# phi of q before the transpose instead of after it, w1 of the first expert by contraction chunks, and a new written-out order for the first stage of a linear-attention and mixture-of-experts kernel

## The chip, the cores and the metric

The kernel runs on one core of a Trainium2 chip. A core has five engines that run side by side and wait for each other by semaphores: TensorE (PE; matrix products, results in PSUM), VectorE (DVE), ScalarE (ACT), GpSimd (POOL) and SyncE (SP). Transfers between HBM and SBUF are issued by SP, ACT or POOL and carried by 16 DMA engines. The metric is the device time of one execution in microseconds (us); lower is better. Each engine has a list of instructions of its own in the program and works through it in order, so an instruction that waits holds up what stands behind it on its engine.

## The reference

The first half is a linear attention over q, k, v of 8 batches, 8 heads, 576 positions and 64 features; the second is a mixture of 8 experts over the 4608 rows that come out, in which every expert works on every row and a balanced routing matrix weighs them.

```python
def phi(x):
    return np.where(x > 0, x, np.exp(x) - 1.0) + 1.0
q_p, k_p = (phi(q), phi(k))
kv = np.einsum('bhsd,bhse->bhde', k_p, v)
z = np.sum(k_p, axis=2)
num = np.einsum('bhsd,bhde->bhse', q_p, kv)
den = np.einsum('bhsd,bhd->bhs', q_p, z)[..., None] + 1e-06
...
logits = x @ w_gate                       # x: (4608, 512), the attention's output
P = np.exp(logits - logits.max())
for _ in range(8):                        # rows, then columns
    P /= P.sum(1, keepdims=True) + 1e-09
    P /= P.sum(0, keepdims=True) + 1e-09
    P *= N / E
for e in range(8):
    h = np.maximum(x @ w1[e], 0.0)        # 512 -> 1024
    out += P[:, e:e + 1] * (h @ w2[e])    # 1024 -> 512
```

phi(x) is computed as min(exp(x), max(x + 1, 1)): one exp on ACT, one tensor_scalar (add, max) and one tensor_tensor (min) on DVE.

## The kernel before, in words

**Stages.** The attention is done in 16 units, one for each batch and group of four heads; unit n is `att(b, g)`, n = 2b + g. A unit loads its parts of k, q and v as tiles of 128 x 1152 elements (L350; k stays fp32, q and v are cast to fp16 by the transfer), makes phi of k (L360, L364, L368), multiplies it with v in 18 matmuls of a 64-row half of the array each (`kv_ps`, L384) and copies the result into the tile `kvz` (L310 on ACT, L312 on DVE). For q it first transposes: 18 matmuls against the identity (L411), each with 64 columns of weights and 128 moving columns, whose results fill 64 of the 128 partitions of the PSUM tile `att`, so that two of them make one 128 x 128 transpose. Then exp (L415, ACT, reading PSUM), max (L418, DVE, reading PSUM) and min (L421, DVE) make `qpT`, phi of q transposed. From qpT and kvz come the denominators (`att`, L434; ACT then takes Ln, L447, and Exp of the negative, L452) and the numerators (`num_ps`, L434), and their product (L462, DVE) is written to `xT`, the transposed x, in fp16.

The experts work on blocks g of 512 rows, nine of them. For expert 0 the blocks 0 to 4 are done plainly (`unit_plain`, `layer1`): 32 matmuls of 512 columns for x @ w1 (`hq`, L635), relu (L640, L642), 32 more for h @ w2 (`ye`, L863) and a copy of the result (L310, L312, L879, L881). Block 0 does its first four pieces of w1's columns in two halves of the contraction: `jobs` in `layer1` lists pieces 0 to 3 with the first two of four 128-row chunks, then the same pieces with the last two, then pieces 4 to 7 whole. Blocks 5 to 8 of expert 0 and all blocks of experts 1 to 7 but the last use a seven-product scheme (`block7`, `unit`), for which sums of blocks of xT are formed (`x_blocks`, L675 to L680) and stored, with xT itself, to a DRAM tile `xd` (L691, L661, L662), from which later experts read them (L708).

As soon as rows of xT are there, the plain blocks of expert 0 are the work with which PE fills the time that the attention leaves. After the last of the four groups of logits (L478) comes the routing: eight iterations on DVE with one small matmul each (L517), also beside expert 0. 46 matmuls of zeros (`yw`, L551) run at the very start; they compute nothing that is used.

**Order.** `_Plan` is a planner inside the kernel: every step is added with an engine, a cost, dependencies and the buffers that it takes, and the planner emits the instructions. For the first stage the planner does not choose: `_FRONT` is a list, written out by hand or by a search, of step numbers with a letter for the engine (p PE, a ACT, d DVE, g POOL, s SP, m a transfer, n nothing), and the steps are emitted in that order. After the list's end it picks by earliest start and priority. Dependencies that the planner knows order the emission only; what an instruction waits for on the chip follows from the tiles that it reads and writes.

**Buffers and queues.** k, q and v have three buffers each (`NK`, `NQ`, `NV`), so a load of unit n waits until the readers of the buffer's previous content are done: for q those are the transposes (PE), for v the 18 kv matmuls (PE), for k the exp and max (ACT and DVE). All loads but the first k go through POOL's queue, in order, with at most eight under way (`p_sw`): the ninth waits for the landing of the first. `att` has two PSUM banks, shared by transposes, denominators, logits and the small routing matmuls; `kv_ps` and `num_ps` share one buffer. The weights of expert 0 are loaded in two parts each (L287): w1 by halves of its 1024 columns, each half in two transfers of 64 partitions, w2 by halves of its contraction. The stores of block sums of the first five blocks (L691) leave from two halves of the tile `acc6` (`p_xse`).

Of the kernel before, what the change touches and what calls it, by code (L numbers as in the profile page):

```python
# [11 lines left out]
FP16 = mybir.dt.float16  # L12
AF = mybir.ActivationFunctionType
ALU = mybir.AluOpType
# [3 lines left out]
class _Plan:  # L18
# [121 lines left out]
    1n 102g 103m 117n 106n 583n 48s 49m 2p 3p 50g 51m 4p 52g 53m 5p 6p 75g 76m 7p 8p 79g 80m 9p 10p 77g 78m 55d 54a  # L140
    11p 12p 124g 125m 13p 14p 15p 0g 16p 56d 17p 18p 126g 127m 19p 20p 21p 61n 107g 108m 62p 109g 110m 22p 63a 23p
    24p 57n 151g 152m 58p 64d 65d 25p 59a 26p 81a 27p 153g 154m 60d 82d 66p 28p 29p 67a 83d 30p 128g 129m 31p 32p 68p
    84n 85p 69a 88n 112g 113m 89p 86d 87a 90a 71p 131d 155g 156m 33p 34p 35p 70a 36p 91d 37p 38p 114g 115m 39p 40p
    92d 130a 41p 42p 43p 72d 93p 178g 179m 44p 94a 45p 73p 46p 74d 137n 95p 111n 180g 181m 96a 132d 100p 47p 97a 138p
    182g 183m 158d 584p 139a 101d 585p 586p 118g 119m 157a 587p 140d 98p 99d 164n 165p 133n 121g 122m 159d 134p 166a
    141d 205g 206m 588p 135a 167d 590p 136a 592p 589d 160n 207g 208m 142p 591d 161p 143a 168d 116n 209g 210m 144p
    162d 594p 145a 163d 596p 234g 235m 185d 146a 169p 597d 147p 598p 170a 148d 236g 237m 600p 184a 599d 595d 171p
    238g 239m 149p 172a 602p 186d 191n 593a 150d 187n 192p 620n 603d 188p 193a 120n 104g 105m 606p 189d 173a 194d
    604p 195d 190a 601a 176p 123n 261g 262m 196p 177d 605p 197a 607p 612d 211a 263g 264m 212d 198p 174p 199a 608p
    213d 218n 290g 291m 200a 175d 219p 265g 266m 214n 215p 220a 621p 216a 221d 292g 293m 217a 240a 623p 222d 622d  # L150
    201p 614a 223p 609p 202d 224a 241d 624a 203p 225p 247n 625p 204d 317g 318m 226a 242d 228p 227a 232p 243n 627p
    626a 229d 233a 267a 268d 248p 230p 249a 319g 320m 629p 231d 274n 344g 345m 296a 610p 250d 321g 322m 251d 244p
    628a 616a 630d 275p 297d 611p 276a 346g 347m 269d 348g 349m 631p 270n 245a 277d 371g 372m 246a 633p 323a 278d
    252p 632d 271p 253a 634a 254p 272d 294g 295m 635p 255a 273d 324d 641p 256a 653n 325d 279p 257p 280a 654p 258d
    636a 281p 618d 259p 282a 656p 655d 303n 326n 283a 260d 304p 657d 284p 305a 402g 403m 298d 642p 400g 401m 285d
    639p 649a 306d 286p 330n 287d 299n 331p 307d 300p 332a 373g 374m 658p 301d 377a 302d 660p 333d 350a 351d 308p
    327p 661d 309a 334d 659a 310p 431g 432m 640p 328d 311a 378d 427g 428m 662p 312a 329d 481g 482m 352d 315p 335p
    664p 316d 336a 647a 313p 337p 314d 357n 637p 338a 569d 638p 339a 663d 340p 358p 341d 665d 643p 359a 342p 666p
    360d 384n 353n 343d 385p 361d 354p 386a 668p 404g 405m 355a 387d 645a 456g 457m 644p 356a 667d 669a 375g 376m
    570d 362p 379d 686n 687p 363a 571d 651a 670p 388d 572s 573m 688a 367p 364p 689p 365a 672p 366a 691p 406a 368d  # L160
    673p 548d 692a 380n 369p 680a 288p 370d 413n 407d 381p 289a 433a 408d 454g 455m 414p 382d 409n 549d 676p 415a
    429g 430m 383d 434d 483g 484m 671p 487a 416d 677p 417d 690a 389p 555d 410p 390a 435d 391p 411d 693p 392a 412d
    678d 396p 393a 418p 550d 695p 419a 397d 674p 556d 420p 557d 394p 421a 675p 558s 559m 395d 440n 436n 551s 552m
    422a 461d 441p 560s 561m 694d 437p 442a 696d 574s 575m 697p 438d 458g 459m 439d 485g 486m 699p 443d 698a 425p
    700a 398p 426d 444d 701p 399a 684a 682a 445p 719n 423p 446a 720p 424d 467n 460a 447p 488d 452p 703p 490g 489d
    448a 538n 544n 539g 540m 705p 462d 449a 541g 542m 702d 463n 468p 545g 546m 453d 706p 469a 450p 721a 722p 470d
    495n 491n 451d 724p 471d 496p 464p 497a 704p 723a 498d 465a 726p 725d 466a 713d 472p 492p 499d 473a 727d 474p
    493a 728p 562d 475a 494a 563d 709p 476a 711d 500p 576d 477p 501a 710p 478d 502p 729d 479p 503a 707p 480d 504a
    708p 505p 715a 730p 506d 732p 717d 577d 507p 731d 733a 742p 508d 734p 536n 756d 509p 763n 578d 757d 736p 735d
    510a 752d 737p 758d 753d 759s 760m 537p 744a 553s 554m 764p 754d 740p 765a 755d 778p 511d 768p 743p 769a 770p  # L170
# [21 lines left out]
    749d 1156a 1163p 1136d 1165p 1135d 1164a 1161p 1132d 1126a 1167p 1166d 1162a 1127g 1200p 1168d 1202p 1201a 1125g  # L192
    1137p 1203a 1169p 1139d 1199n 1206p 1138d 1170a 1254s 1255m 1208p 1207a 1171d 1204p 1175p 1172d 1177p 1173d 1176a
    1205a 1174d 1180p 1178d 1179d 1210p 1181a 1185p 1211d 1188p 1187d 1186d 1212p 1209d 1214p 1213a 1216p 1215a 1191p
    1217a
"""


# [914 lines left out]
```

## Time and profile before

| | us |
|---|---|
| median of the timed runs (three: 972.72, 970.70, 972.14) | 972.14 |
| the profiled execution | 972.0 |
| its span, first to last instruction | 970.2 |
| PE busy in the span | 957.8 (99%) |
| DVE, ACT, POOL busy | 774.8, 566.0, 145.6 |
| PE idle in the first 200 us | 6.6 |
| last load of q, k or v landed at | 113.8 |
| first matmul of expert 1 | 198.2 |

The span and what lies around it make the profiled execution's time; a sum that is made against the profile therefore starts from 972.0. Busy PE is not PE at its peak: a matmul is counted from its start to its modelled end and overlaps the next. How long a group really holds PE is read from the start of its first matmul to the start of the next group's first.

### The profile page before, as it was taken

The numbers are of one execution on the slowest core, as the hardware profiler recorded it, in microseconds if no ns is written. First come the engines' busy times: TensorE is split into PE (matmuls) and PEld (weight loads), VectorE is DVE, ScalarE is ACT, GpSimd is POOL, SyncE is SP. The second block draws the span as 40 slices with busy tenths as digits, with TensorE's granted clock in tenths as the row PEclk, the third lists the DMA queues.
The fourth block names the chain that finished last, engine by engine and source line by source line (L and its number), as shares of the span: only waits on it lengthen the run. The fifth ranks groups of instructions, "written<-read, shape, count | busy, mean of one in ns | idle before, by whom it ended". The sixth has DMA issues, their size and how long they took to land.

```text
span 970.2 us, 21138 instructions
## 1 busy us (share of the span) xinstructions
PE 957.8 (99%) x8624; PEld 796.5 (82%) x8624; DVE 774.8 (80%) x1481; ACT 566.0 (58%) x1004; POOL 145.6 (15%) x209
## 2 busy tenths in 40 slices
PE   8999999999999999999999999999999999999998
PEld 4555566688888888888888888888888888888886
DVE  5897888887887888878887888878887888877775
ACT  6896745555655555555555555555555555555553
POOL 6432100002112111111112111111112111111110
PEclk9999999999999999999999999999999999999999
DMA  9997665023526322272226322272225322236554
GB/s 215 257 227 164 150 179 185 1 77 95 146 77 130 106 74 73 74 160 74 74 76 141 95 74 77 76 161 77 77 77 134 106 78 76 77 99 164 163 164 109
DMA packets 46193, 112.52 MB, mean 116 GB/s; under 512 B 4368, under 2 KB 26640, under 8 KB 46096
## 3 DMA queue, kind: packets, MB, share of 16 engines
q1 hardware_dynamic: 21056, 75.57, 24.0%
q0 software_dynamic: 24640, 35.07, 19.2%
q8 instruction: 67, 1.10, 0.5%
q10 hardware_dynamic: 400, 0.52, 0.2%
q14 instruction: 30, 0.25, 0.1%
HBM read 119.69 MB, written 17.69 MB: 142 GB/s over the span
## 4 chain that ended last, share of the span: by engine, by line
PE 90%; DMA 4%; DVE 3%; ACT 1%; issue 1%; POOL 1%; DVEq 0%; ACTq 0%; POOLq 0%
PE ye L981 33%; PE hq L757 23%; PE att L757 12%; PE Zye L757 6%; PE ye L863 6%; PE Zye L981 5%; DMA vv<-in_v_dram 4%; PE hq L635 2%; PE kv_ps L384 1%; DMA kin<-in_k_dram 1%; DVE h L792 1%; PE att L411 1%; DVE acc L995 1%; PE att L434 1%; PE num_ps L434 1%
## 5 line engine op out<-in xcount | busy, mean ns | idle before, releaser
L995 DVE SCALAR_TENSOR_TENSOR acc<-ye,P_sb,acc 128x256 f32<-128x256 f32 x620 | 267.4, 479 | 125.5 <-PE ye L981 124.9
L757 PEld LDWEIGHTS <-W 128*128 128x128 f16 x2144 | 209.7, 98 | 29.1 <-issue 2.2
L981 PEld LDWEIGHTS <-S 128*128 128x128 f16 x1984 | 193.9, 98 | 23.9 <-DVE S L954 1.4
L1005 POOL TENSOR_TENSOR acc<-acc,st 128x256 f32<-128x256 f32 x124 | 88.1, 730 | 701.1 <-ACT st L1002 583.3
L981 PE MATMUL ye<-T,S 128*128 128x256 f16 x1488 | 192.8, 273 | 0.2 <-DVE S L954 0.2
L757 PEld LDWEIGHTS <-w 128*128 128x128 f16 x1608 | 157.3, 98 | 21.1 <-issue 0.8
L789 ACT ACTIVATE h<-hq 128x512 f16<-128x512 f32 x134 | 80.1, 598 | 149.3 <-PE hq L757 146.0
L981 PEld LDWEIGHTS <-h 128*128 128x128 f16 x1488 | 145.6, 98 | 17.4 <-issue 0.5
L757 PE MATMUL att<-xs,W 128*128 128x256 f16 x1008 | 151.2, 273 | 0.4 <-DVE h L792 0.2
L757 PE MATMUL hq<-xs,W 128*128 128x256 f16 x1008 | 151.2, 273 | 0.0
L757 PE MATMUL hq<-xs,w 128*128 128x256 f16 x1008 | 140.9, 273 | 0.3 <-DVE h L792 0.3
L786 ACT ACTIVATE h<-Zye 128x512 f16<-128x512 f32 x134 | 80.1, 598 | 39.8 <-PE Zye L757 39.8
L792 DVE CUSTOM_DVE_ANT_0 h<-att,s 128x512 f16<-128x512 f32 x126 | 86.6, 687 | 13.1 <-ACT s L776 12.1
L1002 ACT ACTIVATE st<-Zye,P_sb 128x256 f32<-128x256 f32 x124 | 52.3, 470 | 76.2 <-PE Zye L981 76.1
L776 ACT COPY s<-hq 128x512 f32<-128x512 f32 x126 | 73.5, 583 | 35.3 <-PE hq L757 35.2
L954 DVE TENSOR_TENSOR S<-h 128x1024 f16<-128x1024 f16 x124 | 85.2, 687 | 10.9 <-ACT h L789 10.9
L769 ACT COPY Zye<-hq 128x512 f32<-128x512 f32 x134 | 77.8, 581 | 23.3 <-PE hq L757 23.2
L792 DVE CUSTOM_DVE_ANT_0 h<-hq,s 128x512 f16<-128x512 f32 x126 | 86.6, 687 | 3.5 <-PE hq L757 3.3
L863 PE MATMUL ye<-w,h 128*128 128x512 f16 x312 | 76.7, 382 | 0.3 <-DMA w<-in_moe_w_dram 0.2
L783 ACT COPY s<-att 128x512 f32<-128x512 f32 x126 | 74.5, 591 | 2.3 <-PE att L757 1.5
L757 PE MATMUL Zye<-xs,w 128*128 128x256 f16 x504 | 75.6, 273 | 0.0
L981 PE MATMUL ye<-w,S 128*128 128x256 f16 x496 | 64.3, 273 | 0.7 <-DVE S L954 0.7
(102 smaller groups left out, 947.9 us busy)
## 6 DMA issues: line engine op xcount, KB each, us to landing
xs<-xd SPq DMA_DIRECT2D x63, 896.0 KB, 4.6
kin<-in_k_dram POOLq DMA_DIRECT2D x15, 576.0 KB, 8.3
out_dram<-acc SPq DMA_DIRECT2D x67, 128.0 KB, 2.4
w<-in_moe_w_dram POOLq DMA_DIRECT2D x16, 512.0 KB, 8.7
w<-in_moe_w_dram POOLq DMA_DIRECT2D x7, 1024.0 KB, 13.3
qin<-in_q_dram POOLq DMA_DIRECT2D x16, 288.0 KB, 7.4
vv<-in_v_dram POOLq DMA_DIRECT2D x16, 288.0 KB, 8.1
xd<-acc SPq DMA_DIRECT2D x5, 512.0 KB, 3.7
```

The source lines that it names most:

```text
L757: nc.tensor.matmul(dst[:, p, :], lhsT=lhs(p, c), rhs=rhs(c), start=(first and p == 0 and c == 0), stop=(c == 1), skip_group_check=True)
L769: nc.scalar.copy(out=Zt[1], in_=gX["tile"])
L776: nc.scalar.copy(out=gs2["tile"], in_=gX["tile"])
L783: nc.scalar.copy(out=gs5["tile"], in_=gR["tile"])
L786: nc.scalar.activation(out=hd(0, 0), in_=Zt[1], func=AF.Relu)
L789: nc.scalar.activation(out=hd(1, 0), in_=gX["tile"], func=AF.Relu)
L792: nc.vector._custom_dve(TENSOR_ADD_SAT, out=dst, in0=ps, in1=sb, s0=3.0e38, s1=0.0)
L863: nc.tensor.matmul(gy[tt]["tile"], lhsT=gh["tile"][:, f, ds(P * tt, P)], rhs=gw2["tile"][:, f, :], start=(f == 0), stop=(f == NFT - 1))
L954: nc.vector.tensor_tensor(out=Sx[:, i], in0=a0, in1=a1, op=op)
L981: nc.tensor.matmul(bank(g_)[:, s, :], lhsT=lhs(s, kk), rhs=rhs(kk), start=(new and s == 0 and kk == 0), stop=(kk == 3), skip_group_check=True)
L995: nc.vector.scalar_tensor_tensor(out=dst(), in0=bank(g_)[:, s, :], scalar=P_sb[:, gg, e:e + 1], in1=dst(), op0=ALU.mult, op1=ALU.add)
L1005: nc.gpsimd.tensor_tensor(out=dst(), in0=dst(), in1=gst["tile"], op=ALU.add)
```

## The change

Four things change.

1. **phi of q.** exp, max and min are now done on q as it was loaded, [128 x 2 x 9 x 64] in SBUF; the result `tq` holds the two heads of a pair side by side, so that one transpose takes a full 128 x 128 block: nine matmuls for each unit instead of 18. The transposed result is copied from PSUM to `qpT` by ACT or DVE. k's and q's exp share one tile of three buffers.
2. **First w1.** The first expert's w1 is loaded by the four 128-row chunks of the contraction, one transfer of 128 partitions each, in place of the halves of its columns. Block 0's first four half-contraction pieces depend on the first two chunks, all other pieces on all four.
3. **Block sum stores.** In the planner, the store of a block's sums depends on the landing of all loads of q, k and v.
4. **A new `_FRONT`.** The list is replaced as a whole. In the program that comes out, PE does 31 of the 46 zero matmuls before its first other work (before: 20), and POOL issues two more v and q loads ahead of the first w1 transfer, and 14 of the 16 copies to `qpT` are DVE's, two ACT's. From the first blocks of expert 1 on, PE's order is the same in both kernels (13961 of its rows, weight loads counted).

The core of the diff; the planner's cost entries that change with it and the list itself are cut.

```diff
-    1n 102g 103m 117n 106n 583n 48s 49m 2p 3p 50g 51m 4p 52g 53m 5p 6p 75g 76m 7p 8p 79g 80m 9p 10p 77g 78m 55d 54a
+    1n 106g 107m 108n 119n 599n 48s 49m 2p 3p 50g 51m 4p 0g 5p 6p 52g 53m 7p 8p 76g 77m 9p 78g 79m 10p 11p 54a 55d
...
-    p_ek, p_eq, p_t, p_kvz, p_qpT, p_rden = (S_.pool(2) for _ in range(6))
+    p_t, p_tq, p_kvz, p_qpT, p_rden = (S_.pool(2) for _ in range(5))
+    p_ek = p_eq = S_.pool(3)
...
     def load_w1(e, parts=1, **kw):
-        n = F // parts
-        return load_w(moe_w1, "w1", p_w1, [[((slice(64 * r, 64 * r + 64), slice(None), slice(n * i, n * i + n)),
-                                             256 * F * r + n * i, [[F, PW], [PW * F, NDT], [1, n]]) for r in range(2)]
-                                           for i in range(parts)], e, shape=[P, NDT, F], **kw)
+        if parts > 1:
+            return load_w(moe_w1, "w1", p_w1, [[((slice(None), c), PW * F * c, [[256 * F, 2], [F, PW], [1, F]])
+                                                for c in (2 * i, 2 * i + 1)] for i in range(2)], e, shape=[P, NDT, F], **kw)
+        return load_w(moe_w1, "w1", p_w1, [[((slice(64 * r, 64 * r + 64),), 256 * F * r, [[F, PW], [PW * F, NDT], [1, F]])
+                                            for r in range(2)]], e, shape=[P, NDT, F], **kw)
...
+        all_land.extend(tin.values())
...
         def f_qt(_):
             for j in range(NJ):
-                for r in range(2):
-                    nc.tensor.transpose(at2.rearrange("p a b -> p (a b)").bitcast(FP16)[64 * r:64 * r + 64, P * j:P * j + P],
-                                        gin["q"]["tile"][:, r, j, :], ident)
+                nc.tensor.transpose(at2.rearrange("p a b -> p (a b)").bitcast(FP16)[:, P * j:P * j + P],
+                                    gtq["tile"][:, j].rearrange("p r d -> p (r d)"), ident)
...
         def f_qe(_):
-            nc.scalar.activation(out=geq["tile"], in_=qps(), func=AF.Exp)
+            nc.scalar.activation(out=geq["tile"], in_=gin["q"]["tile"], func=AF.Exp)
 
         def f_qm(_):
-            nc.vector.tensor_scalar(out=gq["tile"], in0=qps(), scalar1=1.0, scalar2=1.0, op0=ALU.add, op1=ALU.max)
+            nc.vector.tensor_scalar(out=gtq["tile"].rearrange("p j r d -> p r j d"), in0=gin["q"]["tile"], scalar1=1.0, scalar2=1.0, op0=ALU.add, op1=ALU.max)
 
         def f_qp(_):
-            nc.vector.tensor_tensor(out=gq["tile"], in0=gq["tile"], in1=geq["tile"], op=ALU.min)
...
+            tv = gtq["tile"].rearrange("p j r d -> p r j d")
+            nc.vector.tensor_tensor(out=tv, in0=tv, in1=geq["tile"], op=ALU.min)
+
+        def f_qc(e):
             gq["tile"] = fp.tile([P, 2, NJ, PW], FP16, tag="qpT", name="qpT")
-        t0 = fadd(("none", 0.0), f_qa, deps=[tin["q"], t_id[0]], acq=[gq, geq], prio=pr)
-        t1 = fadd(("pe", 0.626), f_qt, deps=[tin["q"], t0], acq=ga, use=[gin["q"]], prio=pr, cfg=2)
-        t2 = fadd(("act", 1.14), f_qe, deps=[t1], use=[*ga, geq], prio=pr)
-        t3 = fadd(("dve", 0.76), f_qm, deps=[t1, t2], use=[*ga, gq], prio=pr)
-        tq = fadd(("dve", 0.76), f_qp, deps=[t2, t3], use=[geq, gq], prio=pr)
+            copy(e, gq["tile"], qps())
+        gtq = S_.grp(p_tq)
+        t0 = fadd(("none", 0.0), f_qa, deps=[tin["q"]], acq=[gtq, geq], prio=pr)
+        t2 = fadd(("act", 1.16), f_qe, deps=[t0], use=[gin["q"], geq], prio=pr)
+        t3 = fadd(("dve", 0.5), f_qm, deps=[t0], use=[gin["q"], gtq], prio=pr)
+        tm = fadd(("dve", 0.76), f_qp, deps=[t2, t3], use=[geq, gtq], prio=pr)
+        t1 = fadd(("pe", 0.52), f_qt, deps=[tm, t_id[0]], acq=ga, use=[gtq], prio=pr)
+        tq = fadd({"act": 1.13, "dve": 0.76}, f_qc, deps=[t1], acq=[gq], use=[*ga, gq], prio=pr)
...
-            t1 = add(("pe", 0.2175 * (c1 - c0)), f_hq, deps=[tw1[f // 4], prev_hq[0]] + xd_[0:c1 if g == 0 else None],
+            t1 = add(("pe", 0.2175 * (c1 - c0)), f_hq, deps=[tw1[0 if c1 == 2 else 1], prev_hq[0]] + xd_[0:c1 if g == 0 else None],
...
-        ti = add(("sp", 0.45), f_st, deps=[last], use=[gt_], prio=0.0)
+        ti = add(("sp", 0.45), f_st, deps=[last] + all_land, use=[gt_], prio=0.0)
```

## The prediction

> **What bounds the kernel now.** I read the page's first two parts, then the busy time by stretches of the first stage, then the timelines of PE, POOL and SP there, and last the groups of the operations that change. The page first: PE's row, its clock, and DMA.
>
> ```profile
> PE 957.8 (99%) x8624; PEld 796.5 (82%) x8624; DVE 774.8 (80%) x1481; ACT 566.0 (58%) x1004; POOL 145.6 (15%) x209
> ...
> PEclk9999999999999999999999999999999999999999
> DMA  9997665023526322272226322272225322236554
> ```
>
> PE is the bound throughout; from the first blocks of expert 1 (198.2 us) its order is the same in both kernels. So the question is how much earlier or later PE gets there. The stretches of the first 200 us (columns: busy us of PE, PEld, DVE, ACT, POOL, then PE's granted clock, DMA share, GB/s):
>
> ```profile
> 0.00:40.00 40.00, 36.09 (x309) 19.03 (x310) 28.10 (x46) 26.51 (x32) 22.64 (x38) 1.00 1.09 225
> 40.00:70.00 30.00, 29.35 (x320) 17.10 (x319) 25.75 (x40) 27.71 (x37) 10.76 (x15) 1.00 1.10 262
> 70.00:130.00 60.00, 58.60 (x555) 32.75 (x550) 47.83 (x84) 42.75 (x59) 11.02 (x15) 0.97 0.70 146
> 130.00:200.00 70.00, 69.35 (x493) 46.56 (x490) 59.51 (x135) 36.11 (x66) 0.00 (x0) 1.00 0.35 113
> ```
>
> PE is idle for 3.9, 0.65, 1.4 and 0.65 us, 6.6 in all; up to 40 us the DMA engines are full. DVE and ACT have least room at 40 to 70 us, 53.5 of 60. One undisturbed transpose block on PE, and PE's longest wait after the start:
>
> ```profile
> 101.73 1.03 PE L863 MATMUL ye<-w,h 128*128 128x512 f16 x4
> 102.69 0.69 PE L411 MATMUL att<-ident,qin 128*64 128x128 f16 x18
> 103.31 0.92 PE L384 MATMUL kv_ps<-vv,t 64*128 64x192 f16 x18
> ```
>
> ```profile
> 88.81 1.04 PE L478 MATMUL att<-wg_sb,xT 128*128 128x8 f16 x36
> 91.04 1.22 PE L384 MATMUL kv_ps<-vv,t 64*128 64x192 f16 x18 [1.18 <-DMA vv<-in_v_dram]
> 92.18 1.17 PE L411 MATMUL att<-ident,qin 128*64 128x128 f16 x18
> 93.29 3.56 PE L863 MATMUL ye<-w,h 128*128 128x512 f16 x12
> ```
>
> What made that v late (POOL's and SP's queues):
>
> ```profile
> 81.28 0.72 POOL L350 DMA_DIRECT2D vv<-in_v_dram  x1 [7.62 <-PE kv_ps L384]
> 82.00 0.74 POOL L350 DMA_DIRECT2D qin<-in_q_dram  x1
> 82.72 0.74 POOL L350 DMA_DIRECT2D vv<-in_v_dram  x1
> ...
> 84.01 18.69 SPq L691 DMA_DIRECT2D xd<-acc  x3
> ```
>
> POOL stood 7.6 us for a v buffer, then issued three loads at once; a 512 KB block-sum store joined at 84.01. The three landed at 85.62, 88.83 and 90.99, 3.2 and 2.2 us apart, where full queues land one each 1.4 us earlier on. The groups that change, over the first 200 us:
>
> ```profile
> L418 DVE TENSOR_SCALAR qpT<-att 128x1152 f16<-128x1152 f16 x16 | 12.1, 755 | 9.5 <-ACT eq L415 9.3
> L421 DVE TENSOR_TENSOR qpT<-qpT,eq 128x1152 f16<-128x1152 f16 x16 | 12.0, 752 | 0.2
> L364 DVE TENSOR_SCALAR t<-kin 128x1152 f16<-128x1152 f32 x16 | 12.0, 752 | 2.5 <-DMA kin<-in_k_dram 2.4
> L415 ACT ACTIVATE eq<-att 128x1152 f16<-128x1152 f16 x16 | 18.0, 1126 | 12.6 <-PE att L411 12.6
> L551 PE MATMUL yw<-warm 128*128 128x512 f16 x46 | 13.6, 442 | 1.3 <-DVE warm L540 1.3
> L411 PE MATMUL att<-ident,qin 128*64 128x128 f16 x288 | 11.6, 227 | 0.5 <-DVE qpT L418 0.4
> ```
>
> **The change part by part.** *Transposes.* The block starts at 102.69 and the next group at 103.31: 0.62 us for 18. The four 512-column matmuls before it began at 101.73 and hold PE 0.86 (86.84 to 87.70 for such four), up to 102.59: another 0.10 lost on entry. A unit so pays 0.72. Now nine matmuls with 128 moving columns and full weights: at 0.215 for 512 columns, 0.054 each, 0.48 a block. Loading full weights allows more: the logits' 36 matmuls with full weights take 0.88 us, 0.024 each. Lower end: each full one takes as long as the pair it replaces (0.069), 0.62, and the entry stays: no gain. Upper end: 0.48, no entry, 0.24. I take 0.50 without entry, since full-array groups follow each other without such a gap in the rows: 0.22 x 16 = 3.5 us less (0 to 3.8). All of it is PE work, hence on the path.
>
> A rule speaks against this. The Trainium skill ("TensorE: Matmul & The Clock Gate", Part 4) gives about 275 ns for a full 128x128 bf16 transpose in a kernel's context. By that figure as a spacing the nine would take an estimated 2.5 us and the sum would be some 28 us worse; the trace has 227 ns as one transpose's duration too, but starts them 34 ns apart.
>
> *phi of q.* exp stays on ACT (1.126 from PSUM; L360 reads SBUF in 1.157: +0.03). Max reads SBUF in place of PSUM: L364, same form with fp32 input, 0.752, so 0 saved, half of it (0.38) at best. Min is 0.752 as before. The copy is new: on DVE at most the 0.755 that L418 takes for the same PSUM source, on ACT 1.13. So DVE gains 14 x 0.755 = 10.6 us of work less 0 to 6, ACT 2.3; four relu and two copies move from DVE to ACT in the new list (-4.1, +3.5). On PE's path this costs nothing while other PE work stands between a transpose and its denominator: at least an hq block and a num (1.1 us) in the new order, mostly 2 to 4 us, against 0.1 + 0.755. Without that cover each unit shows up to 0.76. What leaves the path: between transpose and denominator lay 1.126 + 0.755 + 0.752; the two att banks come free earlier, and a q buffer waits no more for PE (POOL's 11.5 us of waits for att go).
>
> *Start.* Issue for issue: 31 zero matmuls end at 10.4 (20 ended at 8.0, a later one takes 0.216), so the first kv starts at 10.5 instead of 9.51 and the first denominator, after the copy, at about 13.2 instead of 12.09. POOL makes the identity ahead of its second load (0.55 later) and puts v2 and q3 before w1 (0.7 of POOL each); behind w1, k of unit 3 lands at 25.9 instead of 21.45 and its kv comes at 28.4 instead of 27.68. With 1.4 us a load, w1's first two chunks (512 KB each, priced 1.4) land at 20.3 and 21.7, all four at 24.5; before, the first half landed at 20.17, all at 28.42. PE comes to its first hq at 22.1 instead of 21.51, but with unit 2's kv done (0.9 us, before at 24.54). w2's halves land at 34.3 and 37.0 (before 35.40 and 37.95, and PE waited 0.18 there). At the kv of unit 5, PE is 1.4 us further on, of which the transposes are 1.0: 0.4 gained. Between -1 and +1.5: the chunks could land as slowly as the 2.04 and 2.09 apart of the old ones.
>
> *Store behind the last load.* This holds in the planner alone. On the chip SP waits for DVE's sums and nothing else, so the first store leaves when DVE has made them, still beside the last v loads; what is stored is first read for expert 1, whose work starts at 198 us. I cost it at nothing; a collision costs the load behind it up to 2.6 us (3.2 + 2.2 - 2 x 1.4). DVE's fourth and fifth early sums wait for a store's landing (3.7 us), with over ten DVE instructions between.
>
> *Stalls.* The wait before 91.04 cost 1.3 us. Behind it the clock was halved for 3.4 us (the profile's 0.97): kv 1.14 to the next start instead of 0.86, the block 1.11 instead of 0.62 and 0.2 of gaps, twelve ye 3.39 instead of 2.58: 1.8. The new order has its own such place: units 9 and 10 use the same v buffer one after the other. Between their kv groups PE has 5.9 us; a load takes 4.2 to 4.9 when POOL's queue is quiet (63.63 to 67.85, 70.74 to 75.63), and up to two loads at 1.4 go ahead: 4.9 to 7.7, so a wait of 0 to 1.9, and with a halved clock 1.8 more. I take 0.9 for the wait and 1.8 for the clock, net 0.4 gained; the ends are 3.1 gained and 1.5 lost.
>
> The Trainium skill (same page, Part 1) says that an idle stretch of about 3.4 us halves the clock. By that a wait of 1.2 us would cost itself alone, and this term would be 2.2 gained. Here 0.9 us of 8-column matmuls and 1.2 idle were enough, so the row decides.
>
> *Sum.* 3.5 + 0.4 + 0.4 = 4.3. The profiled execution's 972.0 becomes 967.7; the median is 0.14 above it: **967.8**.
>
> **The rivals.** *No long wait at all* (every v early): 972.1 - 3.5 - 0.4 - 3.1 + 0.5 for small ones = 965.6. For it: q loads are freed from PE, so POOL's queue moves earlier. Against: the shared v buffer.
>
> *Eaten by the new order:* the wait at units 9 and 10 in full (1.9 + 1.8 against the old 3.1) and as much as 3.5 us of PE waits for tq, which now has to be ready before the transpose instead of after it: 972. For it: an in-order PE has one more DVE result to wait for in each unit. Against: q lands well ahead once its buffer goes free early.
>
> *Slower, DVE and ACT become the bound of the attention.* They are 89% busy at 40 to 70 us; some 4.3 units fall there, and a copy of 0.755 each makes 56.7 of 60. In two in-order engines at 94% each late item waits for PE and PE for it. The 16 copies are 12.9 us; if two thirds come out as PE idle, +8.6 - 3.9 = 976.8, if all, 981. It decides from a third on (4.3 us). Against: over 70 to 130 us the two have 29 us free, the new order moves work to ACT, and DVE's 9.3 us of waits for exp and ACT's 12.6 for the transposes are gone.
>
> *The transposes do not run side by side with their own latency:* nine at 227 ns, 2.04 instead of 0.72, x16: 993. Against: the 34 ns of today. The Trainium skill's 275 ns, named above, is the rule behind it.
>
> That the store change does nothing on the chip is in the sum already.
>
> **How the numbers follow.** A measurement of this kernel can tell about 0.2% (1.9 us) from no change. The forecast (965.9 to 970) has 0.48, no long wait 0.20, eaten 0.13, slower 0.17, slow transposes 0.02. Faster 0.68, same 0.13, slower 0.19. The range reaches from the best ends (3.8 + 1.5 + 3.1 = 8.4 less, 963.7) to 975.5, inside the slower case, leaving out its upper half and the last one; within it, the forecast's own is 965.9 to 970.
>
> **What would show it.** Right: transposes at nine in about 0.50 us with no gap ahead; DVE's waits for exp fall; first hq near 22; expert 1's first matmul near 194; few PE waits over 0.5 us after 40 us. Wrong: PE waiting for DVE's tq or qpT in most units (slower case); a wait for v at units 9 and 10 with the clock at half behind it; w1's chunks landing past 24.5; transposes more than 0.06 apart.

## The result, and the profile after

The changed kernel takes 980.92 us (median; 979.93 to 982.14) where the kernel before, on the same chip, takes 971.88. The ratio is 1.0094 with a 95% interval of 1.0077 to 1.0112: 9.0 us slower, against a forecast of 967.8 and a range that ended at 975.5. The profiled execution took 979.93, its span is 978.2.

The page of the changed kernel, the lines that answer to those of before, and the count of DMA packets (before: 46193 packets, 4368 of them under 512 B):

```profile
PE 956.6 (98%) x8480; PEld 796.8 (81%) x8480; DVE 775.9 (79%) x1489; ACT 569.8 (58%) x1012; POOL 147.1 (15%) x209
...
PEclk9799999999999999999999999999999999999999
...
DMA packets 49264, 112.51 MB, mean 115 GB/s; under 512 B 7952, under 2 KB 29200, under 8 KB 49168
```

PE is busy for 1.2 us less in a span that is 8.0 longer, the second slice of the clock is at 7 tenths, and there are 3584 more packets of under 512 B. The stretches of the first 200 us (columns as before: busy us of PE, PEld, DVE, ACT, POOL, then PE's granted clock, DMA share, GB/s):

```profile
0.00:40.00 40.00, 28.88 (x201) 14.81 (x202) 21.18 (x36) 22.49 (x26) 20.13 (x34) 0.87 1.05 197
40.00:70.00 30.00, 29.90 (x265) 17.08 (x263) 26.61 (x45) 27.65 (x37) 12.48 (x17) 1.00 1.05 222
70.00:130.00 60.00, 59.08 (x528) 34.16 (x526) 53.03 (x93) 48.30 (x68) 13.66 (x18) 1.00 0.80 178
130.00:200.00 70.00, 69.55 (x500) 45.94 (x499) 56.91 (x129) 35.08 (x66) 0.00 (x0) 1.00 0.34 117
```

From 40 us on PE has less idle time than before in every stretch (0.1, 0.9 and 0.45 us against 0.65, 1.4 and 0.65). The loss sits in the first 40 us, where PE is idle for 11.1 us instead of 3.9 and the clock is at 0.87. PE's timeline there (start, us, instruction; in brackets the idle time before it and what ended it):

```profile
22.28 0.41 PE L445 MATMUL num_ps<-qpT,kvz 128*128 128x288 f16 x2 [0.75 <-ACT kvz L313]
29.69 1.04 PE L646 MATMUL hq<-xT,w 128*128 128x512 f16 x2 [7.00 <-DMA w<-in_moe_w_dram]
30.52 0.69 PE L445 MATMUL att<-qpT,kvz 128*128 128x288 f16 x2
```

PE waits 7.00 us for the first w1 at its first hq, which stands at about the place that was forecast (22.7; forecast 22.1). Then it works at half clock until 34.87: the two matmuls at 30.52 last 0.69 us where such a pair lasts 0.41 at 22.28. The four chunk transfers were issued at 9.97 to 14.44 and landed at 29.65, 29.97, 30.34 and 32.10; the forecast had 20.3 to 24.5. POOL's queue stands still behind them:

```profile
30.21 0.70 POOL L353 DMA_DIRECT2D qin<-in_q_dram  x1 [8.21 <-DMA w<-in_moe_w_dram]
```

There is a second loss, far from everything that the diff touches by name. Expert 1's first matmul runs at 201.79 (198.22 before, +3.6 us), so the stretch from there to the end, with the same order on PE, is another 4.4 us longer. PE's timeline at its only long wait there, and DVE's behind it:

```profile
263.83 0.60 PE L768 MATMUL hq<-xs,w 128*128 128x256 f16 x4
267.36 1.01 PE L768 MATMUL att<-xs,W 128*128 128x256 f16 x4 [2.92 <-DVE h L803]
268.16 1.91 PE L992 MATMUL ye<-T,h 128*128 128x256 f16 x8
```

```profile
259.30 0.88 DVE L1006 SCALAR_TENSOR_TENSOR acc<-ye,P_sb,acc 128x256 f32<-128x256 f32 x2 [0.25 <-PE ye L992]
262.64 0.69 DVE L932 TENSOR_TENSOR W<-w 128x1024 f16<-128x1024 f16 x1 [2.47 <-DMA w<-in_moe_w_dram]
```

DVE, in order, waits 2.47 us for expert 2's w1 and is late with the relu that PE needs; behind the wait the clock is halved again (1.01 us for what takes 0.60). Expert 2's loads leave POOL at 251.05, behind its eighth block sum; before the change they left at 235.16, behind the sixth:

```profile
250.37 0.73 POOL L1016 TENSOR_TENSOR acc<-acc,st 128x256 f32<-128x256 f32 x1 [4.49 <-ACT st L1013]
251.05 2.33 POOL L289 DMA_DIRECT2D w<-in_moe_w_dram  x3
```

The groups that the change touched came out as costed: max from SBUF 468 ns, the copy 754, min 752, exp 1158.

```profile
L422 ACT ACTIVATE eq<-qin 128x1152 f16<-128x1152 f16 x16 | 18.4, 1158 | 1.9 <-DMA qin<-in_q_dram 1.8
L429 DVE TENSOR_TENSOR tq<-tq,eq 128x1152 f16<-128x1152 f16 x16 | 12.0, 752 | 2.1 <-ACT eq L422 1.8
L315 DVE COPY qpT<-att 128x1152 f16<-128x1152 f16 x14 | 10.6, 754 | 1.9 <-PE att L414 1.7
L425 DVE TENSOR_SCALAR tq<-qin 128x1152 f16<-128x1152 f16 x16 | 7.4, 468 | 1.5 <-DMA qin<-in_q_dram 1.5
```

### The profile page after: what moved, and what is told of

Same layout as the page of the kernel before. It is cut to its first block, busy times and chain, and to the rows that moved or that the text cites. A ratio compares the mean times of both kernels' runs of the same rounds, so it can differ in the third digit from the quotient of the medians.

```text
span 978.2 us, 20907 instructions
## 1 busy us (share of the span) xinstructions
PE 956.6 (98%) x8480; PEld 796.8 (81%) x8480; DVE 775.9 (79%) x1489; ACT 569.8 (58%) x1012; POOL 147.1 (15%) x209
## 4 chain that ended last, share of the span: by engine, by line
PE 91%; DMA 4%; DVE 3%; ACT 1%; issue 1%; POOL 0%; DVEq 0%; ACTq 0%; POOLq 0%
PE ye L992 33%; PE hq L768 23%; PE att L768 12%; PE ye L874 6%; PE Zye L768 6%; PE Zye L992 5%; DMA w<-in_moe_w_dram 3%; PE hq L646 3%; PE att L445 1%; PE kv_ps L388 1%; PE num_ps L445 1%; DMA qin<-in_q_dram 1%; DVE xT L473 0%; PE att L414 0%; PE att L489 0%
## 5 line engine op out<-in xcount | busy, mean ns | idle before, releaser
L992 PEld LDWEIGHTS <-S 128*128 128x128 f16 x1984 | 194.1, 98 | 22.4
L803 DVE CUSTOM_DVE_ANT_0 h<-att,s 128x512 f16<-128x512 f32 x126 | 86.5, 686 | 11.1 <-ACT s L787 10.2
L780 ACT COPY Zye<-hq 128x512 f32<-128x512 f32 x134 | 77.8, 581 | 27.7 <-PE hq L768 27.6
L992 PE MATMUL ye<-T,h 128*128 128x256 f16 x496 | 65.2, 275 | 0.0
```

The costliest lines, as they stand in the source:

```text
L780: nc.scalar.copy(out=Zt[1], in_=gX["tile"])
L803: nc.vector._custom_dve(TENSOR_ADD_SAT, out=dst, in0=ps, in1=sb, s0=3.0e38, s1=0.0)
L992: nc.tensor.matmul(bank(g_)[:, s, :], lhsT=lhs(s, kk), rhs=rhs(kk), start=(new and s == 0 and kk == 0), stop=(kk == 3), skip_group_check=True)
```

## The experiments

All times below are medians; "to before" is the difference to the kernel before in the same series of runs, which is how kernels of different series are compared. The changed kernel stands at +9.0.

### The first wait: the chunk transfers

Three kernels differ from the changed one in nothing but the four transfers of the first w1: column halves as before the change; 128 rows that follow each other; 64 partitions by two chunks. The three added lines are the three kernels, in this order; in the first, each piece of columns waits for its own half again (`tw1[f // 4]`).

```diff
-[[((slice(None), c), PW * F * c, [[256 * F, 2], [F, PW], [1, F]]) for c in (2 * i, 2 * i + 1)] for i in range(2)]
+[[((slice(64 * r, 64 * r + 64), slice(None), slice(n * i, n * i + n)), 256 * F * r + n * i, [[F, PW], [PW * F, NDT], [1, n]]) for r in range(2)] for i in range(parts)]
+[[((slice(None), c), P * F * c, [[F, P], [1, F]]) for c in (2 * i, 2 * i + 1)] for i in range(2)]
+[[((slice(64 * r, 64 * r + 64), slice(2 * i, 2 * i + 2)), 256 * F * r + 2 * PW * F * i, [[F, PW], [PW * F, 2], [1, F]]) for r in range(2)] for i in range(2)]
```

> The changed kernel with one part undone: the first w1 is loaded by column halves, four transfers of 64 partitions as before, at the places in the queue that its chunks had; the new order and phi of q stay. Theory A (the long wait at the first hq, 7.00 us, is the chunk transfers' own slowness): the first half lands near 21 to 23 us, the wait before the first hq falls to 0 to 1.5 us, the half clock at 24.6 to 34.9 us goes with it, and the time is 971 to 974 us (980.9 less 7.0, less 1.8 to 2.6 for the half clock). Rival B (the new order of the loads of q, k and v keeps w1 back, whatever its shape): the first half lands after 26 us, a wait of 4 us or more stays, 977 to 982 us. Both: the wait of 2.92 us at 264 us, if it comes from the late load of expert 2 and not from the start, is still there within 0.5 us.

> The changed kernel with one change to the four chunk transfers of the first w1: the same 128 rows of 2 KB, but 128 rows that follow each other in memory (one level for the partitions) instead of two groups of 64 rows. So expert 0's w1 has its rows in another order and the output is not the reference's; the work and the bytes are the same. Theory A1 (the two levels of the partition pattern make the slow transfer and the 4-byte packets): chunks land by 25 us, the wait before the first hq is under 1.5 us, 971 to 974 us, and the packets under 512 B fall by 3584 to near 4368. Theory A2 (a transfer of 128 partitions or of 2 KB rows is slow whatever the pattern): the chunks land near 30 us, the wait is 5.5 to 8 us, 979.5 to 982 us.

> The changed kernel with the first w1 still loaded by contraction halves, but each of the four transfers takes 64 partitions by two chunks of 1024 columns (128 rows of 2 KB, one level for the partitions) instead of 128 partitions of one chunk. Theory A1 (two levels of the pattern): as in the run with rows that follow each other, the halves land by 25 us, wait under 1.5 us, 971 to 974 us. Theory A3 (128 partitions in one transfer are the slow case): this run is fast and the run with 128 rows that follow each other is slow. Theory A4 (rows of 2 KB are slow in this stretch, in any pattern): both are slow, landing near 30 us, 979.5 to 982 us.

Measured: 971.85 (to before +0.7, ratio 1.0007, interval 0.9997 to 1.0016), 971.47 (+0.3; 0.9995, 0.9983 to 1.0007) and 971.10 (0.0; 0.9995, 0.9986 to 1.0004). In all three the wait of 7 us and the half clock at the start are gone; the first landing is at 21.1 to 21.5 us and the next follow 1.2 to 1.5 us apart, where the prediction priced 1.4. So the new order does not keep w1 back, and neither the 128 partitions nor the 2 KB rows are slow: the one with 128 rows that follow each other has the same rows as the slow one, in one level. Its count of packets and its stretches:

```profile
DMA packets 45680, 112.50 MB, mean 116 GB/s; under 512 B 4368, under 2 KB 25616, under 8 KB 45584
```

```profile
18.00:22.00 4.00, 3.15 (x31) 1.87 (x31) 3.69 (x6) 3.92 (x6) 1.70 (x4) 1.00 1.14 211
22.00:26.00 4.00, 3.25 (x25) 1.93 (x24) 2.15 (x5) 3.43 (x5) 2.42 (x4) 1.00 1.11 285
```

The 3584 extra small packets of the changed kernel (896 for each chunk) are gone, and from 22 to 26 us 285 GB/s arrive; the changed kernel has 205 there, with PE busy for 0.41 us of 4:

```profile
22.00:26.00 4.00, 0.41 (x2) 0.10 (x1) 1.53 (x3) 1.40 (x2) 0.01 (x1) 0.83 1.12 205
```

The wait of 2.9 us at 264 us stayed in all three (3.09, 3.17 and 3.17 us): it is no echo of the first. Its length is not the same in every execution: in the profiled ones of the next three kernels it is 1.78, 1.71 and 1.88 us, with the clock whole behind it. So a difference of one or two us among these kernels may come from there and not from the first w1.

Next, two groups of 64 rows without a gap between them:

```diff
-P * F * c, [[F, P], [1, F]]
+P * F * c, [[PW * F, 2], [F, PW], [1, F]]
```

> As the run whose chunks take 128 rows that follow each other, with the same rows and bytes, but the pattern written as two groups of 64 rows that join without a gap (so again expert 0's w1 has its rows in another order and the output is not the reference's). If writing the partitions in two levels is what makes the slow transfer: 4-byte packets as in the changed kernel (under 512 B near 7952), landing near 30 us, about 9 to 10 us slower. If it needs the gap between the two groups of rows (or the pattern is joined to one level): packets under 512 B near 4368, landing by 25.5 us, 971 to 972 us.

One execution, 968.66 us, 4368 small packets, landings from 21.94 on. Two groups that join are as good as one (or were made one before they reached the chip). What counts is two groups that cannot be joined. Is it the gap, or the number of groups? Two kernels, with four groups and with sixteen:

```diff
-PW * F * c, [[256 * F, 2], [F, PW], [1, F]]
+32 * F * c, [[128 * F, 4], [F, 32], [1, F]]
+8 * F * c, [[32 * F, 16], [F, 8], [1, F]]
```

> The changed kernel with its chunk transfers written as four groups of 32 rows with gaps between them, instead of two groups of 64 (so expert 0's w1 has its rows in another order and the output is not the reference's; bytes, row length and number of rows are the same). Theory N (the number of groups is the number of engines that carry a transfer): of 16 engines 4 carry each chunk, 32 rows each, and if the others each get as many empty 4-byte packets as a carrier has rows, as 14 x 64 = 896 for each chunk in the changed kernel, there are 12 x 32 = 384 for each chunk, 1536 in all, and the packets under 512 B are 5904; four chunks spread over 16 engines instead of 8, so they land near 22 to 27 us, the wait at the first hq is 0 to 3 us, 971 to 976 us. Theory O (any gap between groups makes the slow transfer): landing near 30 us, wait 6 to 8.5 us, 979.5 to 982 us. By a rule of the Trainium skill, in its page "DMA: Bandwidth & Descriptors", a transfer runs on as many engines, up to 16, as divide the size of the slowest dimension of its patterns; that would be Theory N.

> The same with sixteen groups of 8 rows with gaps (again expert 0's w1 has its rows in another order and the output is not the reference's). Theory N: all 16 engines carry each chunk, no empty packets, under 512 B 4368, landing at 21 to 25.5 us, no wait over 1 us at the first hq, 970 to 972.5 us. Theory O: as slow as the changed kernel, 979.5 to 982 us.

Four groups: 977.16 us (to before +5.5), 5904 small packets, which is the count forecast. The page, and the first hq in the timeline, both of the profiled execution, which at 974.27 us was the fastest of four:

```profile
DMA packets 47216, 112.51 MB, mean 116 GB/s; under 512 B 5904, under 2 KB 27152, under 8 KB 47120
```

```profile
26.53 1.31 PE L646 MATMUL hq<-xT,w 128*128 128x512 f16 x2 [3.74 <-DMA w<-in_moe_w_dram]
```

Sixteen groups, with gaps as well: 969.47 us (to before -2.2), 4368 small packets, no wait over 1 us at the first hq. So it is not the gap. The trace does not name the engine of a packet, but the counts come out if the number of groups is the number of engines that carry a transfer, and every engine that carries nothing of it gets as many 4-byte packets as a carrier has rows: 14 x 64 = 896, 12 x 32 = 384, 0 x 8 = 0. The packets in flight agree: 9.0 of the 2048-byte ones at a time from 24 to 28 us in the changed kernel (four chunks on two engines each), 17.7 from 20 to 23 us in the run with one level and 18.5 in the one with four groups. In the first two of these each packet takes 173 ns, so the changed kernel's are not slower one by one, they are fewer at a time. Theory N missed by 0.7 us on the wait and 1.2 on the time with four groups: there the four chunks together use all 16 engines, but if each sits on four of its own, they land together, as they did at 26.5 to 27.6, instead of one after the other, and the first two chunks, which are all that the first hq needs, get no precedence.

The Trainium skill has this as a rule. Its page "DMA: Bandwidth & Descriptors", section "Why a DMA increments its semaphore by 16 and not by 1", says that a transfer is spread over the largest number of engines, 16 at most, that divides the slowest dimension of both patterns, and its "Rules for kernel authors" that an outermost dimension of size c below 16 confines a transfer to at most c engines. With 2, 4 and 16 engines by this rule, the counts above come out to the packet.

### What the half clock cost at the start

```diff
+                for _z in range(30 if g == 0 and f == 0 and c0 == 0 else 0):
+                    nc.tensor.matmul(ghq["tile"], lhsT=warm[:, 0:P], rhs=warm, start=True, stop=True)
                 for c in range(c0, c1):
```

> The changed kernel as it is, with 30 matmuls of zeros (128 x 512, some 6.4 us) put on TensorE just before the first hq, into the bank that this hq then starts anew: they fill the wait for the chunks and change nothing else. Theory F (the half clock from 24.6 to 34.9 us is a cost of its own beside the 7 us of waiting): the clock stays whole, the time falls by 1.8 to 2.6 us to 978.0 to 979.2 us. Rival G (behind the wait nothing is bound by TensorE, or the matmuls push hq back): 980.3 us or more.

978.02 us (to before +6.4): the clock stays whole over this stretch and 2.7 us are won back, a little more than theory F had (1.8 to 2.6). Of the 9.1 us that the slow transfers cost (+9.0 against 0.0 with 64 partitions by two chunks), 2.7 are the clock that fell during the wait and 6.4 the wait.

### The second wait: expert 2's loads

The planner follows the written list to its end and only then chooses. Expert 2's loads are in neither list, so they are emitted behind the last listed step; the new list reaches two POOL sums further. Here they are put into it:

```diff
-    1138d 1169p 1142a 1137d 1144p 1140a 1170d 1141g 1168d 1147p 1084g 1145d 1171p 1146d 1143g 1173p 1172a 1175p 1174a
+    1138d 1169p 1142a 1137d 1144p 1140a 1170d 1141g 1168d 1147p 1084g 1145d 1171p 1146d 1143g 1498n 1499g 1501g 1504n 1505g 1173p 1172a 1175p 1174a
```

> The changed kernel with the three loads of expert 2 put into the written order behind the fifth block sum of GpSimd (the one at 233 us) instead of behind its end; nothing else. Theory C (the second loss, a wait of 2.92 us at 264 us with a window of half clock, comes from these loads being queued behind eight sums on GpSimd because the written order ends later): the loads leave at 235 us instead of 251, VectorE's first W of expert 2 no longer waits for a DMA (2.47 us), the wait of 2.92 us falls under 1 us and the half clock at 267 us goes: 976 to 978 us. Rival D (VectorE is late there anyway, by the block sums and the four W): the wait stays over 2 us and the time within 1 us of 980.9. The wait of 7 us at the start stays in both.

(The sum before the loads, step 1143, is the sixth on POOL; the expectation miscounts it as the fifth.) 976.69 us (to before +5.6): 3.5 us faster than the changed kernel. The loads leave at 236.57, and DVE's first W finds its data (no wait in brackets):

```profile
236.57 2.16 POOL L289 DMA_DIRECT2D w<-in_moe_w_dram  x3
```

```profile
253.84 0.68 DVE L932 TENSOR_TENSOR W<-w 128x1024 f16<-128x1024 f16 x1
```

PE's wait of 2.92 us and the half clock there are gone; 0.44, 0.40 and 0.81 us remain at 254 to 262 us. Theory C holds.

### Both mended, and the rest of the change

The transfers of e3 and the loads of e5 together; then the same with the loads behind the second block sum (`1027g`).

> The changed kernel with both causes taken away: first w1 in contraction halves of 64 partitions by two chunks, and expert 2's loads in the written order behind the fifth block sum. If the two causes are all that stood against the prediction, the two gains add (9.8 and 4.2 us from 980.9): 966.2 to 968 us, some 4 us below the kernel before, with expert 1's first matmul at 193 us (198.2 before) and no wait over 1 us on TensorE between 30 and 960 us. If they share a cost, or one only moves the other: 969 us or more.

> As the run with both causes taken away, but expert 2's loads stand behind the second block sum instead of the fifth, so that they leave near 200 us instead of 226. If the small waits that were left at 254 to 262 us with the loads at 236 us (0.44, 0.40 and 0.81 us) still come from the third load (landed at 254 us): 0.8 to 1.8 us faster than that run. If they are VectorE's own (block sums, S and W in its queue): within 0.6 us of it; if the earlier loads slow the transfers of x, slower.

968.23 us (to before -3.4; ratio 0.9967, 0.9954 to 0.9979) and 968.17 (0.9965, 0.9953 to 0.9978). The two gains add (9.1 and 3.5 alone, 12.5 together; the time is 0.2 above the range expected), PE has no wait over 0.80 us behind the first 30 us, and expert 1 starts at 194.10. Both kernels beat the one before. The still earlier loads bring nothing: the small waits stay to the hundredth (0.44, 0.40, 0.80), so they do not come from these loads; the profile puts the first two down to ACT and the third to DVE. The first stretches with both mended:

```profile
0.00:40.00 40.00, 35.74 (x260) 18.43 (x261) 27.49 (x46) 28.48 (x36) 22.01 (x38) 1.00 1.09 231
40.00:70.00 30.00, 29.92 (x266) 17.30 (x265) 27.49 (x46) 27.87 (x38) 12.11 (x16) 1.00 1.10 257
70.00:130.00 60.00, 59.08 (x543) 34.48 (x541) 53.16 (x97) 43.95 (x63) 10.25 (x14) 1.00 0.71 154
```

On this kernel the other parts can be weighed. First the transposes, back to 18 halves:

```diff
-                nc.tensor.transpose(at2.rearrange("p a b -> p (a b)").bitcast(FP16)[:, P * j:P * j + P],
-                                    gtq["tile"][:, j].rearrange("p r d -> p (r d)"), ident)
+                for r in range(2):
+                    nc.tensor.transpose(at2.rearrange("p a b -> p (a b)").bitcast(FP16)[64 * r:64 * r + 64, P * j:P * j + P],
+                                        gtq["tile"][:, j, r, :], ident)
```

> As the run with both causes taken away, but phi of q is turned by 18 transposes of 128 x 64 per unit, as before the change, instead of 9 of 128 x 128; the rest of the new path (natural layout, copy) stays. Theory of the prediction (TensorE sets the pace of the front, 0.22 us more per unit): 2.5 to 3.8 us slower than that run, 969 to 971 us, and expert 1's first matmul some 3 us later. Rival H (in the front another engine is as late, the transposes hide): less than 1.2 us slower.

968.80 us (to before -2.9): 0.6 us slower, not 2.5 to 3.8, so rival H holds. The two ratios to the kernel before, 0.9972 (0.9962 to 0.9982) and 0.9967 (0.9954 to 0.9979), overlap: the 0.6 itself is hardly clear of noise. Two lines each of the kernel with nine full transposes, then of that with 18 halves:

```profile
78.12 0.67 PE L415 MATMUL att<-ident,tq 128*128 128x128 f16 x9
78.72 0.92 PE L389 MATMUL kv_ps<-vv,t 64*128 64x192 f16 x18
```

```profile
78.39 0.69 PE L416 MATMUL att<-ident,tq 128*64 128x128 f16 x18
79.02 0.67 PE L389 MATMUL kv_ps<-vv,t 64*128 64x192 f16 x12
```

Ahead of a kv group nine full transposes hold PE 0.60 us and 18 halves 0.63: kv uses half the array's rows, and the 0.10 lost where full and half groups meet has only moved from the block's entry to its exit. Elsewhere the block is 0.50 and the entry 0.10 shorter. Counted from the start of the last matmul ahead of the block to the first behind it, a unit saves 0.22 us, the forecast figure, but 10 of the 16 units have a kv group as neighbour and save 0.12 or less: 2.1 us of PE's time in all, from 15.36 to 13.29. And only some 0.6 of the 2.1 reaches the end: the wait of 0.59 us for DVE's xT at 102.48, for one, is there with full transposes and not with halves.

Then the copy of phi of q, which the prediction costed at nothing, made twice, and with a second pass of the same length that leaves the att bank alone:

```diff
             copy(e, gq["tile"], qps())
+            copy(e, gq["tile"], qps())
```

> As the run with both causes taken away, with the copy of phi of q out of the att bank made twice in a row on the same engine (0.75 us more on VectorE in 14 units, 1.13 on ScalarE in 2). It holds the att bank of each unit some 0.75 us longer, near the 2.86 us from the first transpose to the last reader that the traces show before the change (1.85 after), and adds 12.8 us of engine time. Theory K (what the front gained is the shorter hold of the att bank: one copy reads it where exp and max did): 2 to 4 us slower than the run without the second copy. Rival L (the engines' load counts, not the hold): slower, but no more than the run whose second pass reads SBUF. Rival M (both have room, the copy is covered as the prediction had it): within 0.7 us.

```diff
             copy(e, gq["tile"], qps())
+            if e == "act":
+                copy(e, gq["tile"], gq["tile"])
+            else:
+                nc.vector.tensor_tensor(out=gq["tile"], in0=gq["tile"], in1=gq["tile"], op=ALU.min)
```

> As the run with both causes taken away, with a second pass of the same length over phi of q on the same engine, which reads and writes it in SBUF (a min of it with itself on VectorE, a copy onto itself on ScalarE), so that the att bank is free after the first copy as it is without the pass; the load of the engines and the delay of phi of q are those of the copy made twice. Theory K (the hold of the bank): at least 1 us faster than the copy made twice, within 1 us of the run without a second pass. Rival L (load and delay): as slow as the copy made twice within 0.5 us, 1 us or more slower than without. Rival M: all three within 0.7 us.

976.79 and 976.71 us (to before +5.5 and +5.4): 8.9 and 8.8 us slower than without the second pass, and alike. The hold of the att bank is not what counts (theory K falls: 2.68 us a unit in the one, 1.86 in the other), and the second pass is not covered (rival M falls); what remains is the engines' load and the delay of phi of q (rival L). Of 12.8 us of added work 8.8 come out as time. A unit's wait, from the timeline of the kernel whose second pass is in SBUF:

```profile
49.61 0.41 PE L450 MATMUL att<-qpT,kvz 128*128 128x288 f16 x2 [0.60 <-DVE qpT L438]
```

Waits for qpT of 0.29 to 1.21 us stand at seven places there; with one copy there is one, 0.42 us at 13.4. By an estimate from the two times, the cover over the one copy is some 0.25 us a unit thick on average: (12.8 - 8.8) / 16.

Last, where the front's gain (expert 1 at 194.1 instead of 198.2) comes from. The guess was the wait for v at 89.7 us and the half clock behind it, so in the kernel before the change two groups of ye matmuls were moved ahead of it:

```diff
-    673p 548d 692a 380n 369p 680a 288p 370d 413n 407d 381p 289a 433a 408d 454g 455m 414p 382d 409n 549d 676p 415a
-    429g 430m 383d 434d 483g 484m 671p 487a 416d 677p 417d 690a 389p 555d 410p 390a 435d 391p 411d 693p 392a 412d
+    673p 548d 692a 380n 369p 680a 288p 676p 671p 370d 413n 407d 381p 289a 433a 408d 454g 455m 414p 382d 409n 549d 415a
+    429g 430m 383d 434d 483g 484m 487a 416d 677p 417d 690a 389p 555d 410p 390a 435d 391p 411d 693p 392a 412d
```

> The kernel before the change, with two groups of four ye matmuls of TensorE's written order moved ahead of the kv matmuls that wait 1.18 us for v at 89.7 us; nothing else moved. Theory I (what the changed kernel's front gains is above all this wait and the window of half clock behind it, 1.2 + 1.8 us, not the transposes): 1.5 to 3 us faster than before, 968.7 to 970.2 us, no half clock near 90 us, expert 1's first matmul at 195.2 to 196.7 us instead of 198.2. Rival J (the wait is taken up again by a later wait in the front): within 0.8 us of the kernel before.

971.61 us (to before -0.2; 1.0001, 0.9991 to 1.0010). Wait and half clock are gone from there, and nothing is won: 4 us later PE waits for the next late thing, DVE's max that reads an att bank.

```profile
93.03 1.04 PE L863 MATMUL ye<-w,h 128*128 128x512 f16 x4
95.52 0.41 PE L434 MATMUL att<-qpT,kvz 128*128 128x288 f16 x2 [1.45 <-DVE qpT L418]
```

Theory I fell. Which part of the remaining gain of about 2.9 us is the new order's and which that of phi of q made ahead of the transpose stays open: the list is written for the new path, and no run here parts the two.

## Why the prediction was wrong

**Start (failed; the step that decided).** "With 1.4 us a load, w1's first two chunks land at 20.3 and 21.7, all four at 24.5." The price was taken from transfers whose partitions are one level and held for all such (1.2 to 1.5 us apart, from 21.1 to 21.5 us on). The changed pattern puts a dimension of 2 in front, and its transfers run on two engines each: first landing at 29.65. The term was -0.4 with ends of -1.5 and +1; the slow transfers alone put 9.1 us on top of it (+9.0 with them, 0.0 with those of 64 partitions by two chunks), 6.4 for PE's wait and 2.7 for the clock behind it, for which the term had nothing. The worst end was the spacing of the old transfers, 2.04 and 2.09, again rows of one-level patterns. No row of the trace had this pattern, so no row bounded it; the diff showed the 2, and the rule of the Trainium skill's page "DMA: Bandwidth & Descriptors" named above was there to be weighed. Of the prediction's signs of being wrong, this one came, "w1's chunks landing past 24.5"; the others did not.

**What the new order moves past its end (not in the sum).** The prediction compared the orders up to expert 1 and took what follows as the same, since PE's order is. POOL's is not: expert 2's loads slid behind two more sums because the list ends later. 3.4 to 3.5 us.

**Transposes (mechanism right, size wrong).** 0.22 a unit holds away from kv groups; 0.12 beside them. 2.1 us instead of 3.5 on PE, and 0.6 in time: that all of it lies on the path was wrong; the wait for DVE's xT that takes its place says that DVE is nearly as late as PE in the front. (The 28 us that the prediction gives for transposes of 2.5 us a unit are counted from the kernel before, 2.48 - 0.72 for 16 units; from its sum, which has 3.5 gained, they are 31.6.)

**phi of q (right, with less room than it looked).** One copy costs one wait, 0.42 us at 13.4. The slower rival, DVE and ACT as the bound, gave 976.8 to 981 and so nearly the measured time, but it is not what happened: PE waits for qpT nowhere else. It was close, though. A second copy set it off at once, and two thirds of the added work came out as time, as that rival's lower end had it. Max from SBUF fell between its two bounds (0.468).

**Stalls (net right by luck).** The wait for v at units 9 and 10 did not come; PE runs through 85 to 92 us without one. But the price of the old one, 3.1, was not a gain to be had by itself: covering it alone gave 0.2. The term's lower end, 1.5 lost, does not follow from the terms beside it: 1.9 + 1.8 - 3.1 is 0.6.

**Store behind the last load.** The first store of a block sum leaves at 99.76 instead of 84.01, still ahead of the last load's issue at 102.50, and the next two at 118.69 and 120.82, behind it. No run undoes this part alone: nothing shows that it cost or won anything.

**The sum.** With both causes taken away the kernel needs 968.2, 3.4 less than before, where 967.8, 4.3 less, was forecast. That is agreement of the total, not of the terms: -0.6 from the transposes instead of -3.5, and about -2.9 from order and shorter chain instead of -0.8.

## What to carry to other kernels

Read a transfer's pattern from the outside: if its slowest dimension is 2 and the two groups cannot be joined, the counts here say that it runs on two of 16 engines, and the packets under 512 B on the page tell so (14 empty ones for each row that a carrier moves). Where an order is written out by hand and a planner takes over behind it, look at what comes first after the seam on every queue, not on the bounding engine alone. And a wait is worth what lies between it and the next late thing, not its own length.

## What the runs showed that was not expected

**The clock's windows lie on a fixed grid.** All changes of the granted clock in a run are multiples of 3.413 us apart (24.63 and 266.98 us in the changed kernel are 71 of them). So one wait can cost its length alone or, with a window of 3.41 us at half clock behind it, 1.7 us and more on top, by where it falls. A wait of 3.09 us inside one window (the kernel with column halves; stretches cut on the grid):

```profile
254.47:257.88 3.41, 1.25 (x12) 0.97 (x10) 3.41 (x8) 1.29 (x3) 0.00 (x0) 1.00 1.05 174
257.88:261.29 3.41, 2.48 (x12) 1.76 (x12) 2.07 (x4) 0.59 (x1) 0.00 (x0) 0.50 0.01 1
261.29:264.71 3.42, 3.42 (x18) 2.42 (x16) 2.05 (x4) 1.18 (x2) 0.00 (x0) 0.50 0.37 86
```

and one of 3.17 us over two windows (64 partitions by two chunks):

```profile
253.75:257.17 3.42, 1.99 (x19) 1.64 (x17) 2.98 (x6) 1.75 (x3) 0.00 (x0) 1.00 1.23 206
257.17:260.58 3.41, 1.67 (x16) 1.50 (x16) 3.04 (x7) 0.59 (x1) 0.00 (x0) 1.00 0.07 11
260.58:263.99 3.41, 3.41 (x34) 3.05 (x32) 3.22 (x7) 2.24 (x4) 0.00 (x0) 1.00 0.58 198
```

PE busy for 37% of a window halved the next one; 49%, and 45% in the run with sixteen groups, did not. A window at half clock needed more to be the last: the one with 73% above was followed by another at half, one with 89% in the changed kernel (266.98 to 270.39) was not. The window of the kernel before with 65% that was followed by a half one holds 0.9 us of 8-column matmuls, so not all busy time seems to count alike. The Trainium skill ("TensorE: Matmul & The Clock Gate", Part 1) gives the window as free-running and 3413 ns long, which these runs agree with; that an idle stretch of about 3.4 us is needed, as the prediction read the page, they do not.

**Four carriers each are not 16 in turn.** With four groups the chunks used as many engines as with sixteen and all had landed 2 us later; but the first one came 4.8 us later (26.48 instead of 21.65), and the first is what PE waits for.
